# Where the last second-layer steps, the slots and two halves of weights stand ahead of an expert loop, and which branch is hinted

## The chip, the cores and the metric

One core of a Trainium2 chip runs the program. The metric is the device time of one execution in microseconds; lower is better. The times of the kernel before are a median and an interval of three timed runs, and beside them stands one profiled execution, from which all rows come.

## The reference

Attention of 8 batches with 8 heads, 576 queries and head size 64 over keys and values that are first averaged in groups of 8 (72 keys), then a mixture of experts over the 4608 tokens of width 512. Tokens with a skip score of 0 or less pass through.

```python
k_p = k.reshape(B, H, Sp, pool, D).mean(axis=3)          # v_p alike
scores = scale * np.matmul(q, k_p.transpose(0, 1, 3, 2))
attn = np.exp(scores - max); attn = attn / (attn.sum(-1) + 1e-9)
x = (attn @ v_p).transpose(0, 2, 1, 3).reshape(B * S, H * D)
do_compute = x @ w_skip > 0
e_idx = argmax(xc @ w_gate); gate_w = softmax(xc @ w_gate)[e_idx]
h = np.maximum(xc[mask] @ w1[e], 0.0)                    # for each of 8 experts
y[mask] = gate_w[mask, None] * (h @ w2[e])
out[do_compute] = xc + y
```

## The kernel before

A product in full precision is made of three products of rounded halves: a high half (`whi`, `xhi`, `hhi`, written by ScalarE) and a low half, the rest (`wlo`, `xlo`, `hlo`, written by VectorE or GpSimd). TensorE multiplies high by high, high by low and low by high. A low half of h is an operation of L512, a low half of a chunk of weights one of L555 (`low`).

The program has two stages. The first goes over 36 tiles of 128 tokens: attention, scores of the gate, and a table in memory that collects the tokens of each expert (the writes of L393, issued by GpSimd). Beside it, the tokens of one expert that are already known (two tiles) go through both of its layers: `products` takes the steps of its second layer one at a time, 16 of them at the end. A step is the three matmuls of L523 to L525 of 512 columns; eight steps (k from 0 to 7) fill one of two banks, psF[0] and mb. GpSimd's own list of small work is `gps`, a planner (`Paced`, L606 on) which in each slot of time picks between table writes and other work by due times; its constants say how many writes may stand in a row (L623). `later_low` (L646) numbers the 16 low halves of the weights and gives those up to 12 to it; the other three go to `rest`: VectorE makes 13 and 14 at a stop of `slots` (`late_lows`) and 15 behind the barrier (`lows`).

At the end of the first stage `slots` (L934) works out, on VectorE, which rows of the table belong to which unit of the second stage. It is a generator with stops. Its first part ends with the column of rows (L995) and the gather of these rows by GpSimd (L996), and stops with "". Its second part (from L1000) works out the kind (width) and ends of each unit, puts them through two small matmuls (L1020) and stops with "lows". Then the results are copied, and after another stop the gathered rows are transposed (L1028) and copied to `slot` and `gate` (L1029 on). What stands at the stops is in the loop over `slots` (L914 on): `products(.., 16)` goes on until 16 steps are left, `evacuate` writes halves of h that are waiting, `late_lows` are the two low halves of weights, and each `psum()` (that is, `spare`, L906) takes a bank and fills the time with KEEP = 6 matmuls that nobody reads (L909). The last call leaves SPARE = 10 steps over; they are handed to `experts`.

`experts` opens (L1059) with a barrier (`tc.tile_critical`) that every engine enters. Behind it each engine has a program of its own, with counted semaphores: `P` waits for a semaphore and takes from it, `V` adds. GpSimd gathers three tiles of tokens in the order of PLACES (2, 1, 0; L1182) and signals land2, land1, land0. TensorE runs the ten steps that are left, with steps 2 to 5 ahead of 0 and 1 (`steps[:6] = ...`), waits for the semaphore "lo" ahead of step 5, and behind steps 5, 6 and 7 (BETWEEN) transposes one tile of x each (L1339). ScalarE and VectorE split it into xhi (L1355) and xlo (`x_low`, L1395). VectorE's result of the two early tiles is `early` (L1389).

The units of the loop have one of five widths: 256, 288, 320, 352 or 384 columns. `far_width` (L1125) makes a copy of the first layer, `first`, for each width (96 matmuls, L1274 to L1276), behind a row of four compare-branches (L1132): if kind < 3, go to copy 0; if kind < 4, go to copy 1; and so on. In the code the copy stands right behind its branch, so a test that fails jumps over a copy. Each branch is given a hint: a mark at an earlier place in the instruction stream, from which the branch is announced. `widths_ahead` (L1148) sets such a mark under a test of the register that holds the kind of the unit to come; for the first unit it is called behind step n of 3, for the others in `tx`. The branch at the end of a copy (L1142) has a mark at the head of the copy.

At the very start, WARM = (24, 64) are 24 rounds of two small matmuls (L560) ahead of the first scores.

## Time and profile before

| | us |
|---|---|
| median of three timed runs | 503.99 (503.57 to 505.11) |
| profiled execution, its own time | 502.38 |
| its span on the core | 500.6 |
| PE busy | 478.2 |
| VectorE (DVE) busy | 291.8 |
| ScalarE (ACT) busy | 232.3 |
| GpSimd (POOL) busy | 214.2 |

The profiled execution takes 1.8 us more than its span, and 1.6 us less than the median of the timed runs. Times in rows are counted from the start of the span. The mean granted TensorE clock of the execution is 0.988 of full speed. PE is the array, PEld its loads of weights, PEq and PEldq the sequencer's own instructions; L1065 is the helper that all counted waits share, so the line of a wait is found from what follows it.

### The profile page before, as it was taken

The page shows a single profiled execution, that of the slowest core. Times are in us where ns is not written, and L with a number is a line of the kernel's source. Part 1 is how long each engine was busy: PE and PEld are TensorE (multiplying, and loading weights), DVE is VectorE, ACT ScalarE, POOL GpSimd, SP SyncE. Part 2 cuts the span into 40 slices and gives each one's busy share as a digit, 9 for nine tenths or more (in the row PEclk, how much of TensorE's full clock was granted, in tenths as well). Part 3 has the DMA queues.
Part 4 walks back from the last instruction along what each step waited for, and adds up shares of the span by engine and source line. Part 5 has one row for each costly group of instructions (what it writes and reads, how often), then busy time and mean ns, then how long its engine had stood idle before and what let it go on. Part 6 is the DMA issues. An engine that isn't in the chain of part 4 may idle for free. (4 is left out here: it accounts for less than half of the span.)

```text
span 500.6 us, 10706 instructions
## 1 busy us (share of the span) xinstructions
PE 478.2 (96%) x3290; PEld 437.8 (87%) x3291; DVE 291.8 (58%) x738; ACT 232.3 (46%) x584; POOL 214.2 (43%) x272
## 2 busy tenths in 40 slices
PE   7999899999999989999999997999999999999994
PEld 6899899898888779898989897989899898989893
DVE  4877988888697433566665758733556553322321
ACT  5668678897781023364544547522335242212110
POOL 3489369789886321152304023522022223323221
PEclk9999999999999989999999998999999999999998
DMA  8999799975511165557562637642415120101101
GB/s 252 379 388 392 307 352 388 340 250 192 192 65 44 36 231 210 190 178 270 167 231 85 201 130 263 238 142 63 151 74 180 64 62 21 63 21 60 40 3 39
DMA packets 35364, 87.04 MB, mean 174 GB/s; under 512 B 7246, under 2 KB 9550, under 8 KB 33536
## 3 DMA queue, kind: packets, MB, share of 16 engines
q1 hardware_dynamic: 27392, 71.62, 40.5%
q0 software_dynamic: 7936, 14.99, 8.9%
q8 instruction: 16, 0.26, 0.2%
q14 instruction: 20, 0.16, 0.1%
HBM read 73.25 MB, written 20.73 MB: 188 GB/s over the span
## 5 line engine op out<-in xcount | busy, mean ns | idle before, releaser
L1274 PE MATMUL psl<-xhi,w1hi 128*128 128x256 f32 (+3 forms) x384 | 113.3, 295 | 2.2 <-PEq L1065 2.2
L1275 PE MATMUL psl<-xlo,w1hi 128*128 128x256 f32 (+3 forms) x384 | 113.0, 294 | 0.0
L1276 PE MATMUL psl<-xhi,w1lo 128*128 128x256 f32 (+3 forms) x384 | 113.0, 294 | 0.0
L1187 POOL DMA_INDIRECT out<-ring,slot x36 | 37.3, 1035 | 157.0 <-POOLq L1065 154.5
L1365 ACT ACTIVATE hhi<-psl 128x256 fp32r<-128x256 f32 (+3 forms) x96 | 39.3, 409 | 118.4 <-ACTq L1065 114.2
L1423 DVE SCALAR_TENSOR_TENSOR hlo<-psl,hhi 128x256 fp32r<-128x256 f32 (+2 forms) x96 | 40.4, 422 | 64.3 <-DVEq L1065 61.6
L1274 PEld LDWEIGHTS psl<-xhi,w1hi 128*128 128x128 f32 x384 | 72.8, 189 | 3.3 <-issue 2.9
L1275 PEld LDWEIGHTS psl<-xlo,w1hi 128*128 128x128 f32 x384 | 72.7, 189 | 0.4
L1276 PEld LDWEIGHTS psl<-xhi,w1lo 128*128 128x128 f32 x384 | 72.7, 189 | 0.0
L285 ACT ACTIVATE e<-sc,mn 128x72 f32<-128x72 f32 x288 | 64.9, 344 | 13.2 <-DVE mn L279 12.9
L1182 POOL DMA_INDIRECT ring<-out,slot x39 | 42.7, 1096 | 23.5 <-issue 19.0
L1355 ACT ACTIVATE xhi<-psd 128x512 fp32r<-128x512 f32 x36 | 19.1, 598 | 70.9 <-ACTq L1065 70.9
L310 PE MATMUL o<-vbd,pT 128*128 128x148 f32 (+1 forms) x312 | 49.3, 298 | 2.5 <-DVE x L332 1.4
L310 PEld LDWEIGHTS o<-vbd,pT 128*128 128x128 f32 (+1 forms) x312 | 38.5, 179 | 5.4 <-ACT pT L297 1.8
L393 POOL DMA_INDIRECT table<-pay,r_di x36 | 35.9, 996 | 16.2 <-DVE p_mx L417 7.5
L1400 DVE TENSOR_TENSOR w2lo<-stage,w2hi 128x1024 fp32r<-128x1024 f32 x28 | 34.4, 1227 | 10.7 <-DVEq L1065 9.1
L1296 PE MATMUL psf<-w2hi,hhi 128*128 128x512 f32 x96 | 38.0, 395 | 0.0
L1297 PE MATMUL psf<-w2lo,hhi 128*128 128x512 f32 x96 | 37.4, 390 | 0.0
L1298 PE MATMUL psf<-w2hi,hlo 128*128 128x512 f32 x96 | 37.4, 390 | 0.0
L1181 POOL COPY ring<-gate 128x1 f32<-128x1 f32 x36 | 10.7, 298 | 58.4 <-DMA out<-ring,slot 49.7
L1297 PE MATMUL mb<-w2lo,hhi 128*128 128x512 f32 x88 | 34.3, 390 | 0.0
L1296 PE MATMUL mb<-w2hi,hhi 128*128 128x512 f32 x88 | 34.3, 390 | 0.0
(245 smaller groups left out, 986.9 us busy)
## 6 DMA issues: line engine op xcount, KB each, us to landing
stage<-in_w SPq DMA_DIRECT2D x64, 512.0 KB, 3.5
out<-x SPq DMA_DIRECT2D x36, 256.0 KB
stage<-in_k SPq DMA_DIRECT2D x7, 1152.0 KB
qt<-in_q SPq DMA_DIRECT2D x9, 512.0 KB
hhi<-in_vm SPq DMA_DIRECT2D x4, 1024.0 KB
hlo<-in_vm SPq DMA_DIRECT2D x3, 1024.0 KB
xhi<-in_q SPq DMA_DIRECT2D x4, 512.0 KB
xlo<-in_q SPq DMA_DIRECT2D x4, 512.0 KB
```

The lines of the kernel that those rows point to most:

```text
L285: nc.scalar.activation(ev[:, h // 2, k0:k0 + SP], sc[:, h * SP:(h + 1) * SP], AF.Exp, bias=mn[:, 4 * i + h:4 * i + h + 1], scale=-1.0)
L310: nc.tensor.matmul(o_[sl, g * 2 * VA:(g + 1) * 2 * VA], pT[:, 2 * a + g, sl], vbd[b % 2][:, 2 * a + g, :], start=(g == 0), stop=False)
L1182: g.indirect_dma_start(ring[:, s % 6, 0:D], None, out, bass.IndirectOffsetOnAxis(ap=slot[:, s:s + 1], axis=0), bounds_check=NTOK - 1, oob_ ...
L1187: g.indirect_dma_start(out, bass.IndirectOffsetOnAxis(ap=offsets, axis=0), ring[:, s % 6, 0:D], None, bounds_check=NTOK - 1, oob_is_err=Fa ...
L1274: t.matmul(ps, whi[0][:, k, w], xhi[:, k, xs], start=(k == 0), stop=False)
L1275: t.matmul(ps, whi[0][:, k, w], xlo[:, k, xs], start=False, stop=False)
L1276: last = t.matmul(ps, wlo[0][:, k, w], xhi[:, k, xs], start=False, stop=(k == 3))
L1296: t.matmul(ps, hhi[:, k, sl], whi[1][:, k, :], start=(k == 0), stop=False)
L1297: t.matmul(ps, hhi[:, k, sl], wlo[1][:, k, :], start=False, stop=False)
L1298: last = t.matmul(ps, hlo[:, k, sl], whi[1][:, k, :], start=False, stop=(k == 7))
L1365: a.activation(hhi[:, f, xs], psL[f % 3][:, xs], AF.Relu).then_inc(sem["act"], 1)
L1423: return v.scalar_tensor_tensor(out[:, f, :], psL[f % 3][:, xs], 0.0, hhi[:, f, xs].bitcast(F32), ALU.max, ALU.subtract)
```

## The change

Six edits, all ahead of the expert loop or at its head.

- Low halves of weights: 11 to 15 go to `rest` in place of 13 to 15. 11 and 12 are then `late_lows` and are made by GpSimd right behind the gather of L996, at the stop ""; 13 and 14 move from VectorE's place ahead of the barrier to its place behind the barrier, ahead of 15.
- At the stop "" the steps go on to 15 left in place of 16, and only then h is evacuated, until three of its halves are left; so the second part of `slots` stands behind the first low half of h. The stop behind L1020 now hands over a bank; there the other halves of h are evacuated, the steps go on to 12, and the fillers stand (KEEP is 4 and they come once).
- SPARE is 11 in place of 10: one more step stands behind the barrier. There steps 3 to 6 come ahead of 0 to 2, the transposes stand behind steps 6, 7 and 8, and the wait for "lo" is met ahead of three steps (n of 4, 5, 6) in place of one.
- `Paced` may put up to three large table writes in a row near the end in place of two.
- WARM is 26 in place of 24.
- The first unit's branches have one hint in place of four: if kind is over 2, a mark behind step n of 3 announces jumps[1].

```diff
@@ -62,11 +62,11 @@
 TWO = 1
 LOOPED = True
 PLACES = 2, 1, 0
-SPARE = 10
-BETWEEN = 5, 6, 7
-KEEP = 6
+SPARE = 11
+BETWEEN = 6, 7, 8
+KEEP = 4
 QUARTERS = 288, 320, 352, 384
-WARM, AGAIN = (24, 64), (42, 40)
+WARM, AGAIN = (26, 64), (42, 40)
 FIRST = [b * S // 128 for b in range(B)]
 SLOTS = 3 * (MAXU + 2)
 NO_TOKEN = 1 << 20
@@ -620,7 +620,7 @@
                     work = next((i for i in self.items if i[2] <= t), None)
                     write = next((i for i in self.writes if i[2] <= t), None)
                     if work and write:
-                        i = work if self.wrote > (t > NT - 7) or work[0] < write[0] and work[0] <= t else write
+                        i = work if self.wrote > 2 * (t > NT - 7) or work[0] < write[0] and work[0] <= t else write
                     else:
                         i = work or write
                     if i is None:
@@ -644,10 +644,10 @@
         rest = []
 
         def later_low(cc, i):
-            if cc * 2 + i > 12:
+            if cc * 2 + i > 10:
                 rest.append(lambda v: low(cc, i, v))
             else:
-                gps.add((now["t"] + 1, NT - 6, NT - 6, NT - 1, NT - 1)[max(cc - 2, 0)], wload(cc + 3) - 1 if cc < 3 else (NT - 3, NT - 1, NT + 9, NT + 9)[cc - 3],
+                gps.add((now["t"] + 1, NT - 6, NT - 6, NT - 1)[max(cc - 2, 0)], wload(cc + 3) - 1 if cc < 3 else (NT - 3, NT - 1, NT + 9)[cc - 3],
                         1.25, lambda: low(cc, i))
 
         def adds(b, ready, last):
@@ -901,27 +901,23 @@
                 clock["pe"] = max(clock["pe"], clock["dve"]) + 0.3
                 clock["dve"] = clock["pe"] + 0.3
         gps.take(NT + 99)
-        banks = []
-
-        def spare():
-            banks[:] = [ps_o.tile([128, 2, 512], F32, name="o")]
-            for _ in range(KEEP):
-                nc.tensor.matmul(banks[0][:, 1], hhi[:, 0, 0:128], whi[1][:, 0, :], start=True, stop=True)
-            return banks[0][:, 0].rearrange("p (i n) -> p i n", i=4)
-
         hhi, late_lows = bufs["hhi"], rest[:2]
         rest[:2] = []
+        spare = lambda: ps_o.tile([128, 2, 512], F32, name="o")
         for wait in slots(tc, nc, c, offs, table, near, bufs, out, fin, ap, spare):
             if wait == "":
-                products(NT * 99.0, 16)
+                for f in late_lows:
+                    f(nc.gpsimd)
+                products(NT * 99.0, 15)
+                while len(waiting) > 3:
+                    evacuate()
+                busy[0] = False
+            elif isinstance(wait, bass.AP):
                 while waiting:
                     evacuate()
                 products(NT * 99.0, 12)
-                busy[0] = False
-            elif wait == "lows":
-                for f in late_lows:
-                    f(nc.vector)
-                products(NT * 99.0, 11)
+                for _ in range(KEEP):
+                    nc.tensor.matmul(wait, hhi[:, 0, 0:128], whi[1][:, 0, :], start=True, stop=True)
             elif wait:
                 held = kinds(nc.scalar, fin["nti"])
             elif busy[0]:
@@ -1015,10 +1011,11 @@
     nc.vector.tensor_tensor(kind, kind, le1, ALU.mult)
     yield
     nc.vector.tensor_reduce(both[:, 0:1], kind, axis=AX.X, op=ALU.add)
-    tp = psum()
+    o = psum()
+    tp = o[:, 0].rearrange("p (i n) -> p i n", i=4)
     for i in range(2):
         nc.tensor.matmul(tp[0:1, 2 + i, 0:SLOTS], both[:SLOTS, i:i + 1], c["ident"][:SLOTS, :SLOTS], start=True, stop=True)
-    yield "lows"
+    yield o[:, 1]
     of_unit = tp[0:1, 2:4, 0:SLOTS].rearrange("p i (u s) -> p i u s", s=3)[:, :, :, 0]
     nc.vector.tensor_copy(nti[0:1, UNITS:2 * UNITS], of_unit[:, 1])
     nc.vector.tensor_scalar(nti[0:1, 0:UNITS], of_unit[:, 0], float(TWO), None, ALU.add)
@@ -1130,7 +1127,8 @@
             for i in range(len(QUARTERS)):
                 froms.append(nc.cur_bb)
                 jumps.append(e.br_cond(kind < TWO + i + 1, f"{name}_go{i}", f"{name}_not{i}"))
-                jumps[i].branch_hint(marks[i])
+                if i in marks:
+                    jumps[i].branch_hint(marks[i])
                 nc.switch_bb(f"{name}_not{i}")
             mark = e.mark_branch_hint_location()
             go(widths[-1])
@@ -1318,20 +1316,21 @@
                         second_short()
 
                 assert len(steps) == SPARE
-                steps[:6] = steps[2:6] + steps[:2]
+                steps[:7] = steps[3:7] + steps[:3]
                 loads = registers(t, nti)
                 held = next(loads)
-                marks, jumps = [], []
+                marks, jumps = {}, []
                 for n, (_, _, f) in enumerate(steps):
-                    if n == 5:
+                    i = int(not 4 <= n < 7)
+                    if not i:
                         P(t, "lo")
-                    i = int(not 4 <= n < 6)
                     m = f(psF[1 - i])
                     if m:
                         m.then_inc(sem["l2"], 1)
                     next(loads, None)
                     if n == 3:
-                        marks = widths_ahead(t, held[1])
+                        with t.If(t.snap(held[1], min_val=0, max_val=TWO + 4) > TWO + 1):
+                            marks = {1: t.mark_branch_hint_location()}
                     if n in BETWEEN:
                         i = PLACES[BETWEEN.index(n)]
                         P(t, f"land{i}")
```

## Rows read from the trace of the kernel before

A timeline's row has: start us, us, engine, line, operation, out<-in, xcount, and in brackets the idle time ahead of it with what released it.

**Rows 1.** page, part 1: busy us (share) xinstructions of each engine
```profile
PE 478.2 (96%) x3290; PEld 437.8 (87%) x3291; DVE 291.8 (58%) x738; ACT 232.3 (46%) x584; POOL 214.2 (43%) x272
```

**Rows 2.** waits of PE: line waited for, total us, times, longest us
```profile
PE psl L1274 <- PEq L1065: 2.2, 1, 2.2
```

**Rows 3.** timeline, PE, around the expert loop's first matmul
```profile
179.17 0.40 PE L525 MATMUL psf<-w2hi,hlo 128*128 128x512 f32 x1
...
181.81 0.60 PE L1274 MATMUL psl<-xhi,w1hi 128*128 128x320 f32 x1 [2.24 <-PEq L1065]
```

**Rows 4.** timeline, DVE: the last low part of x
```profile
179.04 0.69 DVE L1395 TENSOR_TENSOR xlo<-psd,xhi 128x512 fp32r<-128x512 f32 x1 [0.67 <-DVEq L1065]
```

**Rows 5.** lines L1132 and L1142, 140 to 200 us: branches, ns
```profile
L1132 PEldq COMPARE_BRANCH  x3: 79/380/2989, 177.9 to 181.5; - x3
...
L1142 PEldq COMPARE_BRANCH  x1: 2039/2039/2039, 194.8 to 194.8; - x1
```

**Rows 6.** windows behind the gap; columns by engine, then clock, DMA
```profile
181.70:185.10 3.40, 3.29 (x12) 3.33 (x13) 0.00 (x0) 0.00 (x0) 0.70 (x1) 0.50 0.74 233
...
185.10:188.50 3.40, 3.40 (x24) 3.40 (x24) 1.11 (x4) 0.87 (x2) 0.13 (x1) 1.00 1.02 402
```

**Rows 7.** timeline, PE, ahead of the barrier and behind it
```profile
163.21 0.39 PE L523 MATMUL mb<-w2hi,hhi 128*128 128x512 f32 x1
...
165.98 1.52 PE L909 MATMUL o<-w2hi,hhi 128*128 128x512 f32 x6
...
167.43 0.44 PE L1020 MATMUL o<-cfs,s_both 81*1 81x81 f32 x4
...
168.61 0.34 PE L1028 MATMUL o<-cfs,stage 81*128 81x81 f32 x2
...
169.31 0.40 PE L525 MATMUL mb<-w2hi,hlo 128*128 128x512 f32 x1
...
170.71 0.47 PE L523 MATMUL psf<-w2hi,hhi 128*128 128x512 f32 x1 [1.01 <-PE mb L525]
```

**Rows 8.** timeline, DVE, ahead of the barrier
```profile
160.06 0.16 DVE L995 TENSOR_TENSOR s_coli<-s_col 128x1 int32<-128x1 f32 x1
...
160.14 0.68 DVE L512 SCALAR_TENSOR_TENSOR hlo<-sc,hhi 128x512 fp32r<-128x512 f32 x1
...
163.16 1.29 DVE L512 SCALAR_TENSOR_TENSOR hlo<-pt,hhi 128x512 fp32r<-128x512 f32 x2 [2.34 <-ACT hhi L509]
...
166.54 1.28 DVE L555 TENSOR_TENSOR w2lo<-stage,w2hi 128x512 fp32r<-128x512 f32 x2
...
168.99 0.24 DVE L1029 CAST slot<-o 128x81 int32<-128x81 f32 x1 [0.81 <-PE o L1028]
```

**Rows 9.** line L1028, 140 to 200 us: PE's sequencer
```profile
L1028 PEldq EVENT_SEMAPHORE  x1: 51/51/51, 167.0 to 167.0; - x1
```

**Rows 10.** timeline, GpSimd (POOL), ahead of the barrier
```profile
151.71 1.30 POOL L555 TENSOR_TENSOR w2lo<-stage,w2hi 128x512 fp32r<-128x512 f32 x1
...
162.73 1.08 POOL L996 DMA_INDIRECT stage<-table,s_coli  x1 [2.18 <-issue]
```

**Rows 11.** timeline, PE, start of the program
```profile
1.75 5.38 PE L560 MATMUL o<-ring 128*64 128x64 f32 x48 [1.75 <-POOL ring L684]
...
8.95 0.51 PE L273 MATMUL sc<-kbd,qt 128*128 128x144 f32 x2 [0.71 <-ACT kbd L190]
```

**Rows 12.** timeline, PE: sets of transposes for x
```profile
174.92 0.60 PE L1339 MATMUL psd<-cfs,ring 128*128 128x128 f32 x4
...
175.28 0.48 PE L523 MATMUL psf<-w2hi,hhi 128*128 128x512 f32 x1
...
177.54 0.63 PE L1339 MATMUL psd<-cfs,ring 128*128 128x128 f32 x4
```

**Rows 13.** timelines of weight loads (PEld) and ScalarE (ACT)
```profile
161.82 0.19 PEld L502 LDWEIGHTS sc<-xlo,w1hi 128*128 128x128 f32 x1 [1.16 <-issue]
...
162.04 1.09 ACT L509 ACTIVATE hhi<-pt 128x512 fp32r<-128x512 f32 x2 [8.15 <-remote]
```

## The prediction

> **What bounds the kernel now.** I read the busy times first: TensorE (PE) is busy for 478.2 us of a span of 500.6 [rows 1]. Little but PE's idle time can be won, so I read the list of what PE waited for, and then the timeline at the place that the diff touches. One of its two longest waits, 2.2 us, stands at the first L1274, the first matmul of the expert loop [rows 2]. In the timeline the last product ahead of the loop starts at 179.17 and lasts 0.40, and the loop's first matmul starts at 181.81 [rows 3]: 2.24 us of nothing.
>
> The wait is named after the semaphore x of L1065, but x was there: the last x_low on VectorE (DVE) ends at 179.04 + 0.69 = 179.73 [rows 4]. What is late is PE's own sequencer. The view of line L1132 has three compare-branches of the tests that choose a width; they took 0.38, 2.99 and 0.08 [rows 5]. Kind is 3 here (320 columns), so the first two jump over a body of 96 matmuls with their loads and the third falls into the body behind it: the 2.99 is the second test, jumps[1]. Behind the gap the granted clock is 0.50 for 3.40 us: twelve matmuls in that window, 24 in the next equal one [rows 6]. At full clock twelve are 12/24 x 3.40 = 1.70; they took 3.29, so the low level cost 1.59.
>
> Ahead of this lies a barrier that all engines enter (L1059). PE arrives last, at 169.31 + 0.40 = 169.71 [rows 7]; DVE's three copies of the slots start at 168.99 and end by 169.5 [rows 8]. PE is last because of its order, not of data: the rows of the slots landed by 167.0, when PE's sequencer passed its wait for them [rows 9], but their transposes L1028 stand behind six filler matmuls, L1020 and a product, and start at 168.61 [rows 7].
>
> **The change part by part.** The sum is made along PE, from L523 at 163.21 to the barrier, then from the barrier to the first L1274.
>
> *The product that moves behind the barrier (SPARE 10 to 11).* Four steps of the second layer run from 163.21 to 165.98, 0.69 each [rows 7]. One less stands ahead of the barrier: -0.69. Behind the barrier it runs while PE would wait for the gathers and then for the slow branch, so it costs nothing there as long as that branch is slow.
>
> *Fillers, KEEP 6 to 4.* L909 is six matmuls from 165.98, and L1020 starts at 167.43: 1.45/6 = 0.24 with the change to the small matmul in it, about 0.225 without [rows 7]; two less are -0.45. They only fill PE while DVE gets ready, so this counts only if what stands behind them is ready sooner too.
>
> *Second part of the slots behind the first low half.* Today DVE writes the four low halves first and stands idle for 2.34 us ahead of the last two, which end at 163.16 + 1.29 = 164.45; the part lies between these and the two low halves of weights at 166.54, so it takes 2.1 at most [rows 8]. Behind the first low half (ends at 160.82) it runs from there to 162.9 at the latest, inside that idle time. L1020 then stands behind the first product, 163.21 + 0.69 = 163.9, and doesn't wait. L1020 itself stays on PE's path, only earlier in it: 0, between 0 and the -0.44 that it lasts [rows 7].
>
> *Two low halves of weights on GpSimd behind the gather L996.* Two operations leave GpSimd's row of table writes and two leave DVE (1.28 together [rows 8]). On GpSimd one takes 1.30 [rows 10]; without two of them the last writes start earlier, and L996 not before DVE's s_coli, written at 160.06 [rows 8]. L996 starts at 162.73 [rows 10], so it can gain some 1.5 us. That is worth nothing: in its new order PE gets to L1028 at 163.21 + 4 x 0.69 + 0.44 + 4 x 0.225 = 167.3, and the rows landed by 167.0 without it [rows 9]. The new low halves end near 162.73 - 1.5 + 1.08 + 2 x 1.30 = 164.9; the products that need them start at about 165.7 and 167.4. Cost 0, the cover being 0.8 to 2.5 us; if GpSimd were later by more, PE would wait for the rest.
>
> *Order of table writes.* Up to three writes in a row in place of two: the same operations, on an engine that isn't last. 0. *WARM 24 to 26* adds four passes of 5.38/48 = 0.11, 0.45 in all, ahead of a wait of 0.71 for kbd that takes them up [rows 11]. 0.
>
> Sum to the barrier: -0.69 - 0.45 = **-1.14**.
>
> *Behind the barrier.* PE restarts at 170.71, 1.00 after its arrival, and goes through six steps to the first transposes at 174.92, 0.70 each; the third set starts at 177.54 [rows 7, 12]. A set moves PE on by 175.28 - 174.92 = 0.36. With one step more ahead of them the third stands at 170.71 + 9 x 0.70 + 2 x 0.36 = 177.73, 0.19 later against the barrier than now (where it comes later than its own sum, 177.03, and so has a wait in it), and so does x (179.92 on the old scale). PE's sequencer isn't behind its array here: the first of the three tests is reached at 177.9 with transposes and two steps still queued [rows 5]. So the slow branch, not x, still decides, and 1.8 us of it hide the 0.19. The two added waits for "lo" (n of 4 and 5) have behind them only steps on PE; DVE restarts with PE, at about 170.7 on the old scale, and its three low halves at 1.28/2 = 0.64 each [rows 8] are done by 172.7; the first of these waits is met after four steps, at 173.5. DVE's next work, early(0), waits for PE anyway; SP's weight loads wait for DVE's signal behind these halves and for GpSimd's behind the third gather, which comes last (its transposes start at 177.54 [rows 12]).
>
> *The other hint.* Before, four hints name the branch that is logically taken; now one names jumps[1] when kind is over 2, which is the slow one. The bounds: 0 if the code of jumps[1]'s target is asked for no sooner; -2.61 (2.99 to the first test's 0.38 [rows 5]) less what x then limits. The nearest row is the branch of L1142 at the loop body's end: it had a hint 13 us ahead and took 2.04 all the same, 0.95 less than the slow one [rows 5]. That hint stood in the very body whose end it names; jumps[1] is reached right behind the jump of the first test, with hardly time between. I take -0.2.
>
> [...]
>
> Total -1.14 - 0.2 = -1.34. The profiled execution took 502.38 (span 500.6), so it would take 501.04; the three timed runs have a median of 503.99, 1.61 above it, and there the forecast is **502.65**. PE-bound work behind it moves as a whole.
>
> **The rivals.** *B: the hint works.* Then x decides: the first L1274 about 0.3 behind x, 179.92 + 0.3 - 1.14 = 179.1 in place of 181.81 - 1.14 = 180.7, -1.6. PE's gap shrinks to some 0.4, and if the clock then stays up, -1.59 more. 503.99 - 1.14 - 1.6 - 1.59 = 499.65; 501.25 if the clock falls anyway. For it: the hint names the branch that is slow. Against: the 2.04.
>
> *C: a new wait takes the place.* PE and ScalarE show a stop that nothing in the trace releases: a load of weights at 161.82 after 1.16 us of nothing, and ScalarE held for the same matmuls until 162.04 [rows 13]. If such a stop comes in the changed run alone, its 1.2 us eat the gain: 503.9. The other way to C is DVE's second part being held up while GpSimd computes beside it; if it ends 1.3 later (one operation of GpSimd [rows 10]) L1020 and all behind it on PE come up to 1.3 later: again 503.9. Against: it ends by 162.9, when GpSimd's low halves have only begun.
> [...]
>
> *D: slower.* One more code load is exposed. The branch of L1142 takes 2.04 unseen only because matmuls are queued ahead of it [rows 5]. If the loop's head moves in the code so that such a load falls where nothing is queued, it costs 2.99, and -1.34 turns to +1.65: 505.6, or 507.2 with a lowered clock behind it. It decides from the point where PE's instructions ahead of the loop don't cancel: +8 (WARM), -4 (KEEP), -6 (tests and hints), +2 (waits) is 0, which speaks against it.
>
> **How the numbers follow.** Forecast A 0.50, B 0.27, C 0.15, D 0.08. A measurement here tells 0.3% apart, 1.5 us. A's own range is 501.4 to 503.7 (the hint from 0 to -0.95, L1020 from 0 to -0.44, the stop of C in one of the two kernels), and its -1.34 lies just inside the bound: two fifths of A are faster. Faster: 0.20 + 0.27 = 0.47; same: 0.30 + 0.15 = 0.45; slower 0.08. The range takes in A, C and most of B: 499.6 to 504.6.
>
> **What would show it.** PE's arrival at the barrier 1.1 us earlier against the first L523; L1020 behind the first product without a wait; DVE's second part ahead of the second low half; the first L1274 about 12.1 us behind PE's arrival, as now, with a branch of 2.0 to 3.0 at L1132 ahead of it. A branch under 0.5 there and no stretch at 0.50 behind it is B; L1020 waiting for s_both is C. The prediction is wrong if the rows, not PE, end last at the barrier, or if the loop itself changes length.

## The result and the profile after

The changed kernel is slower: 510.73 us, median of four timed runs (510.51 to 511.19), against 504.17 (503.57 to 505.11) for four runs of the kernel before. The ratio is 1.0142, interval 1.0116 to 1.0167. The forecast was 502.65, its range 499.6 to 504.6; the time lies 6.1 us above the upper end. The profiled execution after took 510.55 us, 8.2 us more than the profiled execution before; its span is 508.7. The ratios and intervals, here and in the experiments, leave out executions over 1.5% above the fastest of their kernel (three of nine of `after_two`, one of eleven of `spare13_fill_golate`, and one near 950 us each in `before_hint_golate` and in the kernel before of set 1), whereas the medians count every execution and the ranges leave out only the two near 950.

Part 1 of the page of the kernel after (busy us, share, instructions) answers to [rows 1]:

```profile
PE 477.4 (94%) x3292; PEld 436.0 (86%) x3293; DVE 295.5 (58%) x738; ACT 232.7 (46%) x584; POOL 214.9 (42%) x272
```

PE does the same work and is idle for 8.9 us more. VectorE is busy for 3.7 us more, though the change takes two operations away from its stretch ahead of the barrier and puts as many behind it. The waits of PE in the kernel after (line waited for: total us, times, longest us) answer to [rows 2]:

```profile
PE psl L1272 <- PEq L1062: 3.5, 2, 2.5
PE o L1017 <- DVE s_both L1013: 3.3, 1, 3.3
...
PE psf L1294 <- PEq L1062: 1.3, 1, 1.3
```

The first wait is the old one (L1272 was L1274). The second is new, and it is the one that my rival C named. The third stands at the end of the first loop body. PE's timeline of the kernel after, from the first product to the loop, answers to [rows 3, 7]:

```profile
164.58 0.39 PE L523 MATMUL mb<-w2hi,hhi 128*128 128x512 f32 x1
...
168.74 0.70 PE L1017 MATMUL o<-cfs,s_both 81*1 81x81 f32 x4 [3.31 <-DVE s_both L1013]
169.37 0.80 PE L523 MATMUL mb<-w2hi,hhi 128*128 128x512 f32 x1
...
172.73 1.07 PE L920 MATMUL o<-w2hi,hhi 128*128 128x512 f32 x4
174.16 0.45 PE L1025 MATMUL o<-cfs,stage 81*128 81x81 f32 x2 [0.36 <-DVE nti L1021]
...
176.35 0.47 PE L523 MATMUL psf<-w2hi,hhi 128*128 128x512 f32 x1 [1.00 <-PE mb L525]
...
188.35 0.39 PE L1272 MATMUL psl<-xhi,w1hi 128*128 128x320 f32 x1 [2.54 <-PEq L1062]
```

Why s_both is late stands in the timelines of VectorE and of GpSimd (POOL) of the kernel after; they answer to [rows 8, 10]:

```profile
163.18 0.16 DVE L991 TENSOR_TENSOR s_coli<-s_col 128x1 int32<-128x1 f32 x1
163.26 0.69 DVE L512 SCALAR_TENSOR_TENSOR hlo<-sc,hhi 128x512 fp32r<-128x512 f32 x1
...
164.59 3.31 DVE L1003 TENSOR_TENSOR s_odd<-s_odd,s_three 128x8 int32<-128x8 int32 x1
167.93 0.17 DVE L1005 TENSOR_TENSOR s_none<-s_none,s_odd 128x8 f32<-128x8 f32 x1
```

```profile
164.27 1.07 POOL L992 DMA_INDIRECT stage<-table,s_coli  x1 [2.26 <-DVE s_short L999]
165.37 2.49 POOL L555 TENSOR_TENSOR w2lo<-stage,w2hi 128x512 fp32r<-128x512 f32 x2
176.92 1.60 POOL L1180 DMA_INDIRECT ring<-out,slot  x1 [9.06 <-issue]
```

L1003 works on 8 elements a partition, as its neighbours do, which take 0.17. It took 3.31 and ended at 167.90; GpSimd's two low halves ended at 165.37 + 2.49 = 167.86. In the kernel before the same operation took 0.16:

```profile
165.66 0.16 DVE L1007 TENSOR_TENSOR s_odd<-s_odd,s_three 128x8 int32<-128x8 int32 x1
```

The windows of the kernel after (length; busy time of PE, PEld, DVE, ACT, POOL; granted clock; DMA) show PE's clock behind its wait:

```profile
165.40:168.80 3.40, 0.09 (x2) 0.06 (x2) 3.33 (x8) 0.00 (x0) 2.46 (x2) 0.96 0.15 34
168.80:172.20 3.40, 3.40 (x11) 2.60 (x12) 1.69 (x3) 0.00 (x0) 0.00 (x0) 0.54 0.00 0
172.20:175.60 3.40, 2.79 (x12) 1.67 (x11) 0.72 (x5) 0.00 (x0) 0.00 (x0) 1.00 0.00 0
```

Behind 3.3 us of nothing the granted clock was 0.54 for 3.40 us, and 1.00 in the next window. The three steps from 169.37 to 172.73 took 3.36; at 0.69 a step [rows 7] they take 2.07, so 1.29 is lost there.

The branches of the kernel after, 140 to 205 us (count: shortest/median/longest ns, and when), answer to [rows 5]:

```profile
L1129 PEldq COMPARE_BRANCH  x3: 75/391/3276, 184.2 to 187.9; - x3
...
L1140 PEldq COMPARE_BRANCH  x1: 3759/3759/3759, 201.4 to 201.4; - x1
```

| stretch along the path, us | before | after | more |
|---|---|---|---|
| start to the L390 at 121 us (VectorE's operation that makes a tile's routes) | 121.26 | 121.59 | 0.33 |
| from there to the last L390 | 33.93 | 36.46 | 2.53 |
| last L390 to the first psf product behind the barrier (the restart) | 15.52 | 18.30 | 2.78 |
| from there to the loop's first matmul | 11.09 | 12.00 | 0.91 |
| the loop to the end | 318.76 | 320.38 | 1.62 |

The five add up to 8.17. My sum covered the third and the fourth line: -1.14 and, with the hint, -0.2. From the first L523 to the barrier's other side the third line holds 3.31 (wait at L1017) + 1.29 (clock) + 0.26 (L1017 itself, 0.70 in place of 0.44) + 0.36 (L1025) - 1.14 (the forecast gain) = 4.08 of the 4.27 by which that piece grew. The rest of the line, 1.49 less, lies ahead of the first L523. All of it is the stop of PE [rows 13] that the trace of before has there and this one has not: in before, four steps from one matmul to the next took 1.97 where they take 0.12 each elsewhere.

```profile
160.08 0.28 PE L502 MATMUL sc<-xlo,w1hi 128*128 128x256 f32 x1
...
162.05 0.28 PE L503 MATMUL sc<-xhi,w1lo 128*128 128x256 f32 x1
```

### The profile page after: what moved, and what is told of

It reads as the page before. It is cut to its first block, busy times and chain, and to the rows that moved or that the text cites. A ratio compares the mean times of both kernels' runs of the same rounds, so it can differ in the third digit from the quotient of the medians.

```text
span 508.7 us, 10710 instructions
## 1 busy us (share of the span) xinstructions
PE 477.4 (94%) x3292; PEld 436.0 (86%) x3293; DVE 295.5 (58%) x738; ACT 232.7 (46%) x584; POOL 214.9 (42%) x272
## 5 line engine op out<-in xcount | busy, mean ns | idle before, releaser
L1272 PE MATMUL psl<-xhi,w1hi 128*128 128x256 f32 (+3 forms) x384 | 113.3, 295 | 3.5 <-PEq L1062 3.5
L1274 PE MATMUL psl<-xhi,w1lo 128*128 128x256 f32 (+3 forms) x384 | 113.0, 294 | 0.0
L1185 POOL DMA_INDIRECT out<-ring,slot x36 | 38.5, 1070 | 157.6 <-POOLq L1062 154.8
L1272 PEld LDWEIGHTS psl<-xhi,w1hi 128*128 128x128 f32 x384 | 72.7, 189 | 4.7 <-issue 4.3
L1274 PEld LDWEIGHTS psl<-xhi,w1lo 128*128 128x128 f32 x384 | 72.8, 190 | 0.0
L1294 PE MATMUL psf<-w2hi,hhi 128*128 128x512 f32 x96 | 38.1, 396 | 1.3 <-PEq L1062 1.3
L1294 PE MATMUL mb<-w2hi,hhi 128*128 128x512 f32 x88 | 34.3, 390 | 0.0
```

Source lines behind the costliest of these rows:

```text
L1185: g.indirect_dma_start(out, bass.IndirectOffsetOnAxis(ap=offsets, axis=0), ring[:, s % 6, 0:D], None, bounds_check=NTOK - 1, oob_is_err=Fa ...
L1272: t.matmul(ps, whi[0][:, k, w], xhi[:, k, xs], start=(k == 0), stop=False)
L1274: last = t.matmul(ps, wlo[0][:, k, w], xhi[:, k, xs], start=False, stop=(k == 3))
L1294: t.matmul(ps, hhi[:, k, sl], whi[1][:, k, :], start=(k == 0), stop=False)
```

## The experiments

All kernels of one set ran on the same chip and share the runs of the kernel before, whose medians were 504.10, 502.56, 502.84, 502.62 and 504.09 in the five sets. "Edit" is against the kernel after or before, as the name begins; `dve_lows` and `spare13` are of the kernel after. A ratio is not the quotient of the two medians and can differ from it: `dve_lows_b` has 0.9961, and its medians give 0.9979.

| set | kernel | median (range), us | ratio to before |
|---|---|---|---|
| 1 | after_dve_lows | 505.38 (503.42 to 508.14) | 1.0017 (0.9995 to 1.0039) |
| 1 | after_one_low | 508.13 (504.57 to 510.05) | 1.0074 (1.0049 to 1.0099) |
| 1 | after_shift6 | 511.29 (509.81 to 511.97) | 1.0140 (1.0096 to 1.0184) |
| 1 | before_hint | 508.67 (507.42 to 510.14) | 1.0092 (1.0060 to 1.0125) |
| 2 | dve_lows_two | 502.41 (500.24 to 503.05) | 0.9986 (0.9965 to 1.0007) |
| 2 | before_hint_bare | 503.07 (500.24 to 505.76) | 1.0007 (0.9981 to 1.0033) |
| 2 | before_hint_golate | 506.18 (503.28 to 506.78) | 1.0056 (1.0026 to 1.0087) |
| 2 | before_dead80 | 503.11 (501.89 to 504.47) | 1.0004 (0.9983 to 1.0026) |
| 3 | after_two | 506.10 (499.67 to 508.61) | 1.0003 (0.9960 to 1.0047) |
| 3 | dve_lows_b | 501.80 (500.38 to 503.64) | 0.9961 (0.9938 to 0.9985) |
| 3 | dve_lows_two_b | 501.55 (500.15 to 504.14) | 0.9979 (0.9947 to 1.0010) |
| 3 | spare13 | 502.90 (500.01 to 507.47) | 0.9988 (0.9951 to 1.0026) |
| 4 | after_c | 505.94 (501.89 to 507.38) | 1.0056 (1.0028 to 1.0083) |
| 4 | spare13_fill | 500.70 (499.91 to 502.28) | 0.9957 (0.9936 to 0.9977) |
| 4 | spare13_fill_golate | 502.58 (500.43 to 508.83) | 0.9984 (0.9953 to 1.0014) |
| 5 | before_three | 504.66 (501.57 to 505.34) | 1.0005 (0.9983 to 1.0027) |
| 5 | before_spare11 | 504.76 (503.28 to 506.74) | 1.0006 (0.9987 to 1.0026) |
| 5 | spare13_fill2 | 508.81 (506.24 to 509.83) | 1.0092 (1.0059 to 1.0124) |

### What holds L1003

The theory: GpSimd's two halves of weights hold VectorE's operation on two inputs in SBUF. The rival: the gather ahead of them does it. The first kernel has VectorE make the two halves, behind the second part.

```diff
-                for f in late_lows:
-                    f(nc.gpsimd)
...
+                for f in late_lows:
+                    f(nc.vector)
                 products(NT * 99.0, 12)
```

> The changed kernel, but its two late low halves of weights are made by VectorE, behind the last low half of h, and GpSimd makes none behind the gather. Theory A (GpSimd's two halves hold VectorE's L1003, an operation on two SBUF inputs, for as long as they last): L1003 takes under 0.2 us in place of 3.31, TensorE's wait at L1017 falls from 3.31 to under 1, and no stretch of lowered clock follows it; 510.7 - 2.6 - 1.3 + up to 0.6 for halves that are now made later = 506.2 to 507.4. Rival B (the issue of the gather L992 holds L1003, and the halves only happen to stand behind it): L1003 still takes about 0.75, up to the gather's end; the time is nearly the same, 506.5 to 507.5, so the operation's length tells the two apart. Rival C (a stop that has nothing to do with GpSimd): L1003 still takes about 3 us, 510.7.

VectorE's and GpSimd's timelines of after_dve_lows:

```profile
164.98 0.16 DVE L1003 TENSOR_TENSOR s_odd<-s_odd,s_three 128x8 int32<-128x8 int32 x1
```

```profile
164.75 1.07 POOL L992 DMA_INDIRECT stage<-table,s_coli  x1 [2.31 <-DVE s_short L999]
```

L1003 stands 0.23 into the gather's issue and takes 0.16; in dve_lows_b (below) it stands 0.32 into it, as in after, and takes 0.16 too. The gather alone doesn't hold it, and the rival falls. PE's wait at L1017 went from 3.31 to 1.06, and the ratio from 1.0142 to 1.0017: the one edit that stood at cost 0 in the prediction is worth 1.25%, 6.3 us, by these two ratios, and all the rest of the change together nearly nothing. They come from different sets, though with nearly the same time of before (504.17 and 504.10); how far the size holds is taken up at after_c.

One of the two halves on GpSimd, the other on VectorE:

```diff
-                for f in late_lows:
-                    f(nc.gpsimd)
+                late_lows[0](nc.gpsimd)
...
+                late_lows[1](nc.vector)
                 products(NT * 99.0, 12)
```

> The changed kernel with one of the two late halves on GpSimd behind the gather, and the other on VectorE behind the last low half of h. Theory A (held for as long as GpSimd's halves last): L1003 takes 3.31 - 1.25 = 2.06 us, TensorE's wait at L1017 about 2.1, 510.7 - 1.25 = 509.4, up to 1.3 less if the clock stays up. Rivals B (the gather's issue) and C (neither): L1003 as long as in the changed kernel or as long as with no half on GpSimd, nothing in between.

That L1003 would be held by one half was a miss: the gather came late (165.65), and the second part was done by then. The hold fell on another operation. VectorE's and GpSimd's timelines of after_one_low:

```profile
166.70 1.89 DVE L555 TENSOR_TENSOR w2lo<-stage,w2hi 128x512 fp32r<-128x512 f32 x1
```

```profile
166.75 1.27 POOL L555 TENSOR_TENSOR w2lo<-stage,w2hi 128x512 fp32r<-128x512 f32 x1
```

VectorE's own half, 0.69 elsewhere [rows 8: 1.28 for two], took 1.89, and ended 0.57 behind GpSimd's. So it is not L1003 alone: two different operations of VectorE on two inputs in SBUF were held beside GpSimd's halves, one beside one half for 1.2, the other beside two in a row for 3.15. One that reads an input from PSUM was not held: in after_shift6 (below) GpSimd makes both halves too, but the gather came 0.8 later behind s_coli (1.87 against 1.09), the second part was done by 164.44, and a low half of h took its usual 0.68 beside them. VectorE's and GpSimd's timelines of after_shift6:

```profile
165.57 0.68 DVE L512 SCALAR_TENSOR_TENSOR hlo<-sc,hhi 128x512 fp32r<-128x512 f32 x1
```

```profile
165.08 2.54 POOL L555 TENSOR_TENSOR w2lo<-stage,w2hi 128x512 fp32r<-128x512 f32 x2
```

The length of the hold in the kernel after is 3.15, through two instructions of GpSimd without an end of VectorE's between them, and it starts 0.78 ahead of the first half. These are measured; how one engine holds the other is not shown.

The changed kernel with the old rule for table writes, and the changed kernel once more without any edit:

```diff
-  ... self.wrote > 2 * (t > NT - 7) or ...
+  ... self.wrote > (t > NT - 7) or ...
```

> The changed kernel with the old rule for table writes (two in a row), its two late halves still on GpSimd behind the gather. Theory A (the halves on GpSimd are what costs): it stays some 4 to 5 us slower than dve_lows_two_b on the same chip, near 507, and an operation of VectorE on two SBUF inputs stands held for 1 us or more beside the halves. Theory S (the rule of three is what costs, by delaying the routes and so bringing VectorE's second part beside the halves): most of the loss is gone, 503 to 504, within 1 us of dve_lows_two_b.

> The changed kernel itself once more, on the chip and in the hour of the two kernels beside it. Theory A (the cost is a meeting of GpSimd's two halves with VectorE's second part of the slots, which depends on when the gather L992 comes against that part): where the profile shows L1003, or another operation on two SBUF inputs, held for 2.5 to 3.3 us, TensorE's restart stands 17.5 to 18.5 us behind the last L390, and where none is held, 15 to 16; the runs spread over 3 us or more, as those of after_two did (499.7 to 508.6), with a median 3 to 7 us above the kernel before. Rival S (besides that, the rule of three delays the routes): the last L390 stands 36 us or more behind the routes at 121; without it 32.9, as dve_lows_b showed.

VectorE's timeline of after_two:

```profile
160.83 3.31 DVE L1003 TENSOR_TENSOR s_odd<-s_odd,s_three 128x8 int32<-128x8 int32 x1
```

In after_c it is again 3.31, at 160.51. The first half starts 0.79 behind L1003 in after_two and 0.80 in after_c. In both, PE waits 3.30 at L1017 and the clock falls behind it: the granted clock is 0.74 from 165 to 168.4 us in after_two and 0.50 from 164 to 168 us in after_c. The piece from the last L390 to the restart took 18.46 in after_two and 19.64 in after_c, longer than expected of the latter, since the lower clock lasted for all three steps and the fillers. Against dve_lows_b (0.9961), after_c (1.0056) stands 0.95% higher, 4.8 us, though in another set. after_two scatters from 499.67 to 508.61, and its interval settles nothing by itself: beside dve_lows_two_b of its own set, which differs by the two halves alone (0.9979, 0.9947 to 1.0010), the two intervals overlap, although in the traces the way from the last L390 to the restart is 18.46 against 14.13. Of the kernels that differ by the halves only, and within one set, the times part clearly for after_one_low alone (1.0074 against 1.0017 of after_dve_lows).

The hold itself is shown by the traces. Its size in time is less sure: one and the same kernel stands at 1.0142 in the first comparison and at 1.0056 in set 4, and the two intervals are apart. The halves explain 1.25% and 0.95% by the two pairs; why the first comparison lies 0.9% above set 4 is not shown.

### The head of the loop

The hint alone, in the kernel before; first with five added pairs of semaphore instructions ahead of the loop, then bare:

```diff
-                        marks = widths_ahead(t, held[1])
+                        with t.If(t.snap(held[1], min_val=0, max_val=TWO + 4) > TWO + 1):
+                            marks = {1: t.mark_branch_hint_location()}
...
+                for _ in range(5):
+                    V(t, "pad")
+                    P(t, "pad")
                 units(t, held, unit)
```

> The kernel before with the new hint alone (one, on jumps[1] when kind is over 2, in place of four), and ten instructions of padding ahead of the loop so that the loop's code lies within one instruction of where it was. Theory H0 (the hint does not bring the code sooner): the second test of L1132 still takes 2.9 to 3.3 us, 504.2 within 0.8. Rival H1 (the hint works): under 0.5 us, the gap ahead of the first L1274 shrinks from 2.24 to some 0.5, and with the clock up behind it 504.2 - 1.7 - 1.6 = 500.9.

> The kernel before with the new hint alone and without padding. Theory D (the code that jumps[1] leads to is fetched only when TensorE gets there, and the fetch takes long when the weight loads of SyncE have started first; in before_hint the padding brought TensorE there 0.5 us behind the first packet of the loads in place of 1.0 ahead of it): without padding the branch comes ahead of the loads again, takes 2.9 to 3.3 us as in the kernel before, and the time is 504.1 within 0.8. Rival H (the new hint itself does harm): the branch takes over 4 us again, 507 to 509.

The bare hint gives 1.0007: nothing in time. Its branch took 4.55, and not 2.9 to 3.3 as expected, and started 0.94 behind SP's first load. The profiled execution was the longest of its ten (505.76), PE's clock was low behind the restart (granted 0.50 from 171.0 to 174.4, 1.28 a step in place of 0.69), and so the branch came late. With the pairs the time got worse, which neither theory had; the five pairs take PE's sequencer 1.6 us ahead of the branch. Branches of before_hint, and SP's timeline of it:

```profile
L1132 PEldq COMPARE_BRANCH  x3: 75/391/5758, 179.3 to 185.6; - x3
```

```profile
178.25 4.43 SPq L1168 DMA_DIRECT2D stage<-in_w  x8
```

The slow branch starts at 179.77, 1.53 behind SP's first load of weights. A packet of an instruction queue starts at 183.20, behind those loads; that it holds the code behind the jump is my reading. In the kernel before, branch and loads start together, at 178.42 and 178.41, and such a packet, of 16 KB, starts 0.64 behind the branch. So I formed a second theory: a hint brings nothing, and the price of the jump is set by whether weight loads stand ahead of this packet. The test holds the loads back in before_hint, by moving VectorE's signal "go" behind its last x_low:

```diff
-                v.engine_nop().then_inc(sem["go"], 1)
                 held = kinds(v, nti)
...
                 m.then_inc(sem["x"], 1)
+                v.engine_nop().then_inc(sem["go"], 1)
                 early(1)
```

> The kernel before_hint (new hint and ten instructions of padding), but VectorE's signal that lets SyncE start the weight loads comes behind its last low half of x in place of ahead of the loop, some 1.4 us later. Theory D (the branch's fetch waits behind the weight loads' packets): the fetch starts under 1 us behind the branch, the branch takes 2.9 to 3.3 us in place of 5.76, and the time falls from 508.7 by 2.5 to 3, to some 506; the loads of 4 MB have slack for 1.4 us. Rivals H (the hint) and K (the padding, by its place in the code): the branch takes 5 to 6 us still, 508.7.

Branches of before_hint_golate, and SP's timeline of it:

```profile
L1132 PEldq COMPARE_BRANCH  x3: 75/391/3416, 178.4 to 182.3; - x3
```

```profile
179.58 6.05 SPq L1168 DMA_DIRECT2D stage<-in_w  x8
```

5.76 became 3.42, with the packet 0.69 behind the branch. The ratio fell from 1.0092 to 1.0056, 1.8 us where 2.5 to 3 were expected; with these intervals that difference shows nothing.

The rival to the whole view was that the code behind the jump is asked for ahead of the jump, at a point that depends on where the tests stand in the code. 80 instructions that are jumped over move the tests to another place:

```diff
+                        with t.If(t.snap(held[1], min_val=0, max_val=TWO + 5) > TWO + 4):
+                            for _ in range(80):
+                                V(t, "pad")
```

> [...] Rival F (a block is asked for only by the jump into it): 2.9 to 3.3 us as before, 504.1 + 0.2 for the jump.

The branch took 3.05 with its packet 0.62 behind it, and the time is the same (1.0004). In both places that were tried, 2.99 and 3.05 for the branch, the packet starts behind the branch (0.64 and 0.62) and not ahead of it.

The changed kernel with three pairs ahead of the loop was to show whether the branch at the loop body's end (3.76 in after, 2.04 in before) depends on its place in the code:

```diff
+                for _ in range(3):
+                    V(t, "pad")
+                    P(t, "pad")
                 units(t, held, unit)
```

> [...] The three pairs themselves cost nothing, being behind TensorE's last products and ahead of the slow branch L1129.

The pairs did cost: they take the sequencer 0.95, and the branch at the head came 0.91 behind the first load and took 4.67. That at the body's end no longer stands out (0.38). In its profile L1003 also took only 0.16, and the wait at L1017 was 1.07, so the 1.0140 of this kernel can't be put down to the hold: against the trace of after_dve_lows, the way from the restart to the loop is 2.15 longer and the loop 0.95. The branch at the body's end took 0.38 in dve_lows_two and 3.27 in dve_lows_two_b, which are the same kernel, so its place in the code doesn't decide. What does is open.

### What the rest of the change is worth

The kernel after with VectorE's halves and the old rule for writes, twice; and with the new rule once more:

```diff
-                for f in late_lows:
-                    f(nc.gpsimd)
...
+                for f in late_lows:
+                    f(nc.vector)
                 products(NT * 99.0, 12)
...
-  ... self.wrote > 2 * (t > NT - 7) or ...
+  ... self.wrote > (t > NT - 7) or ...
```

> The changed kernel with its two late low halves on VectorE (as in the experiment after_dve_lows) and with the old rule for table writes, two in a row in place of three. Theory S (the packets of GpSimd's table writes hold back TensorE's completion signals, and the longer rows of writes make more of these stops; in the kernels run so far the last routes L390 stand 33.9 us behind those at 121 with the old rule and 36.0 to 36.6 with the new one): that distance falls from 36.6 to about 34, and the time from 505.4 by up to 2.3, to 503.1. Rival L (it is the two halves that left GpSimd's row, whatever the rule): the distance stays at 36 or more, 505.4. Rival N (the distance is noise): anywhere between 33.9 and 36.6, and the time follows it.

> The kernel dve_lows_two once more, beside dve_lows_b on the same chip. Theory S: 0.3% faster than dve_lows_b; rival N: the same within 0.1%. Against the kernel before: about 0.7 us faster (0.9986 as measured earlier), TensorE's restart behind the barrier 1.3 us earlier against the last L390 and 0.8 of it given back between the restart and the first matmul of the loop.

> The kernel after_dve_lows once more, on the same chip as dve_lows_two_b, which differs by the rule for table writes alone (three in a row here). Theory S: the last routes L390 come 2 us or more later behind those at 121 than in dve_lows_two_b, and the time is 1.5 to 2.5 us longer. Rival N (the difference between the two earlier runs was one of chips): the distance from 121 to the last L390 is the same within 0.5 us, and so is the time.

From the last L390 to the restart these take 14.16, 14.13 and 14.17, against 15.52 before. That is 1.36 less, but it is not the prediction's 1.14: the 15.52 of before holds the stop of 1.5 ahead of the first L523, and from the first L523 to the restart these three take 7.62 to 7.70, against 7.50 before. Nearer neighbours are three kernels that are as before up to the barrier and have no stop in their traces: before_hint_golate takes 15.51 from the last L390 to the restart, before_hint_bare 15.95, before_dead80 16.05. PE waits 1.34 to 1.79 there for the rows of the slots. PE's timeline of before_dead80:

```profile
168.71 0.42 PE L1028 MATMUL o<-cfs,stage 81*128 81x81 f32 x2 [1.79 <-DMA stage<-table,s_coli]
```

Their last table write starts 5.2 to 5.5 behind the last L390 and the gather 4.1 to 4.5 behind s_coli; in the three kernels here it is 3.0 and 1.1. So what the rest of the change brings, 1.3 to 1.9, goes with the earlier rows. PE waits at two new places in them, 0.2 at L1017 and 0.36 at L1025. VectorE's and PE's timelines of dve_lows_b:

```profile
166.99 0.17 DVE L1020 CAST nti<-o 1x27 int32<-1x27 f32 x1 [1.14 <-PE o L920]
```

```profile
167.31 0.45 PE L1025 MATMUL o<-cfs,stage 81*128 81x81 f32 x2 [0.36 <-DVE nti L1021]
```

The copy of the kinds waits for the four fillers, which write to the same tile, and PE waits for the copy. Behind the barrier they take 11.89, 12.08 and 11.73 to the loop's first matmul, against 11.09, so 0.6 to 1.0 is given back. The rule made no difference: from the L390 at 121 us to the last is 32.90 in all three. In time they stand at 0.9961 to 0.9986, and only the interval of dve_lows_b leaves 1 out.

The rule alone, and the step alone that moves behind the barrier (with VectorE's two halves), in the kernel before:

```diff
+  ... self.wrote > 2 * (t > NT - 7) or ...
```

> The kernel before with the new rule for table writes alone (up to three in a row near the end in place of two). Rival N (in an hour without late signals of TensorE the rule changes nothing that counts): the last routes L390 stand 32.9 us behind those at 121, and the time is within 0.8 us of the kernel before. Theory S (the rule delays the routes): 34 to 36.5 us, and 1 to 2.5 us slower; if TensorE's completion signals come late in this hour, as they did in the first session, with more of them than the four in the kernel before.

```diff
-SPARE = 10
-BETWEEN = 5, 6, 7
+SPARE = 11
+BETWEEN = 6, 7, 8
...
-        hhi, late_lows = bufs["hhi"], rest[:2]
-        rest[:2] = []
+        hhi, late_lows = bufs["hhi"], []
...
-                steps[:6] = steps[2:6] + steps[:2]
+                steps[:7] = steps[3:7] + steps[:3]
...
-                    if n == 5:
+                    i = int(not 4 <= n < 7)
+                    if not i:
                         P(t, "lo")
-                    i = int(not 4 <= n < 6)
```

> The kernel before with the moved step alone: 11 steps behind the barrier in place of 10, in the new order, the three last low halves of weights on VectorE behind the barrier in place of one, six fillers as before. Theory X (what stands behind the barrier is paid: the three halves of VectorE hold up GpSimd's first gather behind the barrier, 1.59 us in place of 1.07 as in every kernel with three halves there, and the branch comes later with it): the restart comes 0.6 to 1.2 us earlier against the last L390, the way from the restart to the loop's first matmul is 11.8 to 12.0 us in place of 11.1, and the time is within 0.5 us of the kernel before. Rival Y (as I forecast: the step costs nothing there): that way is 11.1 to 11.3 us, the time 0.7 to 1.1 us shorter.

before_three: VectorE's L390 at 121 us and the last:

```profile
121.07 0.16 DVE L390 TENSOR_TENSOR r_di<-r_ds,mb 128x7 int32<-128x7 f32 x1
...
157.32 0.16 DVE L390 TENSOR_TENSOR r_di<-r_ds,mb 128x3 int32<-128x3 f32 x1 [0.22 <-DMA table<-pay,r_di]
```

That is 36.25, 2.3 more than before, and yet the restart comes only 0.63 later (171.34) and the time is the same (1.0005): this trace has no stop ahead of the first L523.

before_spare11, which has the stop, gains 0.1 ahead of the barrier (15.41; 0.23 from the first L523 on), not 0.69: PE gets there sooner and waits 1.56 there in place of 1.01, because the slots' copies on VectorE now end last. And it loses behind it. GpSimd's and PE's timelines of before_spare11:

```profile
171.67 1.59 POOL L1181 DMA_INDIRECT ring<-out,slot  x1 [7.38 <-issue]
```

```profile
171.10 0.47 PE L523 MATMUL psf<-w2hi,hhi 128*128 128x512 f32 x1 [1.56 <-SPq L1058]
...
183.22 0.38 PE L1273 MATMUL psl<-xhi,w1hi 128*128 128x320 f32 x1 [2.60 <-PEq L1064]
```

From restart to loop 12.12, against 11.09. The first gather takes 1.59. It does so (1.59 to 1.61) in all 14 kernels in which VectorE makes three halves behind the barrier, and takes 1.07 in all 6 in which it makes one: 171.28 in the kernel before, when that one half, 170.63 to 171.32, is all but over. The hold of L1003 would be the other way round here, VectorE holding GpSimd; that the halves are the cause rests on the split of 14 to 6 and on this run.

### More steps behind the barrier

A version of my own: the kernel after with VectorE's halves at the stop ahead of the transposes, 13 steps behind the barrier and the old rule; then (spare13_fill) with five matmuls that nobody reads on PE just ahead of the barrier, in a bank of their own, the last three lines of the diff; then with "go" late as above.

```diff
-SPARE = 11
-BETWEEN = 6, 7, 8
+SPARE = 13
+BETWEEN = 5, 7, 8
...
-                steps[:7] = steps[3:7] + steps[:3]
+                steps[:9] = steps[5:9] + steps[:5]
...
+        bank = ps_s.tile([128, 512], F32, name="sc")
+        for _ in range(5):
+            nc.tensor.matmul(bank, hhi[:, 0, 0:128], whi[1][:, 0, :], start=True, stop=True)
```

> The kernel dve_lows_two with 13 steps of the second layer behind the barrier in place of 11 (transposes behind steps 5, 7 and 8), and the two halves on VectorE behind the copies of the units' kinds. Theory Q (what stands behind the last transposes on TensorE hides the slow branch; two steps more there cost nothing, and two less stand ahead of the barrier, where the gathered rows then bound the time): the restart comes 1.3 to 1.8 us earlier against the last L390 than in dve_lows_two, the way from the restart to the loop's first matmul stays within 0.3 us of 11.9, and the time is 1.2 us less, 0.3% under dve_lows_two_b. Rival R (the two steps are paid behind the barrier, as the one in the changed kernel was): from the restart to the loop 13.2 us, the same time as dve_lows_two_b.

> The kernel spare13 with five more filler matmuls on TensorE behind the transposes L1025, in a bank of their own, so that TensorE is busy until about when VectorE reaches the barrier. Theory G (in spare13 the gap of 2.13 us ahead of the restart brought the clock down, the first five steps behind it took 1.28 us each in place of 0.69, and so the slow branch came 1.2 us behind the first packet of the weight loads in place of 1.0 ahead of it and took 7.55 us): the gap falls to about 1.1, the steps take 0.69 each from the first on, the branch is reached some 0.5 us ahead of the first packet or more and takes 3 to 3.5 us; 502.9 - 3 = 500. Rival V (the two steps behind the barrier are what makes the branch late): the branch is again behind the loads and takes over 4.5 us, 502 to 503.

> The kernel spare13_fill, with VectorE's signal that lets the weight loads start behind its last low half of x in place of ahead of the loop. Theory D (the block of code for jumps[1] waits behind the loads' packets wherever these are first): the fetch starts within 0.8 us of the branch in every profile, the branch takes 3.0 to 3.5 us, the runs spread less than those of spare13 (500.0 to 507.5), and the median is 499.5 to 500.5, 0.5% under the kernel before. Rival W (the loads are needed by then: a later start is paid in the loop): the loop, from its first matmul to the end, is 1 us or more longer than in spare13_fill.

PE's timelines of spare13 and of spare13_fill at the restart and at the loop:

```profile
167.56 0.77 PE L523 MATMUL psf<-w2hi,hhi 128*128 128x512 f32 x1 [2.13 <-SPq L1056]
...
185.81 0.60 PE L1272 MATMUL psl<-xhi,w1hi 128*128 128x320 f32 x1 [4.93 <-PEq L1062]
```

```profile
168.10 0.47 PE L523 MATMUL psf<-w2hi,hhi 128*128 128x512 f32 x1 [1.01 <-PE sc L928]
...
179.76 0.39 PE L1275 MATMUL psl<-xhi,w1hi 128*128 128x320 f32 x1 [0.87 <-PEq L1065]
```

Without fillers PE restarts 0.12 sooner behind the last L390 (13.42 against 13.54) and takes 6.59 longer from there to the loop (18.25 against 11.66). The profiled execution of spare13 took 506.99, and its median is 502.90. Its 2.13 of waiting are followed by steps of 1.28 in place of 0.69 (granted clock 0.50 from 169.4 to 172.8); so the branch comes 2.18 behind the first load (175.70) and takes 7.55. With fillers the steps keep 0.69, branch (176.31) and load (176.28) start together, the branch takes 3.06, and no lower clock follows (1.00 from 179.7 to 183.1). This kernel is the fastest of its set, 0.9957 (0.9936 to 0.9977). Late loads add nothing to it: in the trace the branch takes 3.29 and the loop 322.2 in place of 319.2. That fits a price of the late loads in the loop, but 1.03 of the 3.0 is a longer wait at the first body's end, and the rest is not traced.

The same with the two halves at the earlier stop and four fillers:

```diff
+                for f in late_lows:
+                    f(nc.vector)
                 products(NT * 99.0, 13)
```

> The fastest kernel so far, spare13_fill (0.9957 of the kernel before), with the two late halves of VectorE ahead of the copies of the units' kinds, where VectorE stood idle for 1.2 us, and four fillers behind the transposes in place of five. If VectorE bounds the barrier there: the copies of the slots start 0.4 us earlier against the last L390 and the restart with them, the branch takes 3.0 to 3.5 us ahead of the loads, and the median is 0.9947 to 0.9957 of the kernel before. If the gathered rows bound it instead: the same time as spare13_fill within 0.1%, 0.9957.

It took 1.0092, but its trace has 38.2 from the L390 at 121 us to the last and a wait of PE of 4.4 at L374, well ahead of the edit. So the place of the halves isn't settled by it, and the gain of spare13_fill is shown in one set only, one whose traces have no such waits.

### The routes

The second line of the table of stretches (2.53) was in no term of mine. The signals of PE come late in some traces. Timelines of before and of after, the last transpose and the ScalarE operation that waits for it:

```profile
129.51 0.27 PE L293 MATMUL pt<-cfs,e 128*128 128x128 f32 x1
...
129.88 0.70 ACT L297 ACTIVATE pT<-pt 128x640 f32<-128x640 f32 x1 [0.83 <-PE pt L293]
```

```profile
129.85 0.27 PE L293 MATMUL pt<-cfs,e 128*128 128x128 f32 x1
...
131.22 0.70 ACT L297 ACTIVATE pT<-pt 128x640 f32<-128x640 f32 x1 [1.84 <-PE sc L273]
```

ScalarE starts 0.10 behind the transpose's end in the one and 1.10 behind it in the other. Between 100 and 170 us the semaphore records hold 4 signals of PE over 0.1 us late in before, 9 in after, 9 in before_three and none in after_c; in after, most of them come while packets of GpSimd's table writes are under way. From the L390 at 121 us to the last is 33.93, 36.46, 36.25 and 32.91 in these four. The traces of sets 2 to 4 have no such signals and take 32.9 with either rule; each of those of sets 1 and 5 has 5 or more. Sets 1 and 3 ran on one chip, so the chip alone isn't it. The stop that I put into rival C [rows 13] goes with one of these: the signal of a matmul that ended at 159.06 came at 162.02. before_hint and before_spare11 have the same signal late (161.75 and 162.53) and the same stop.

## Why the prediction was wrong

*What bounds the kernel*: right. PE is the bound, and its gap at the loop's head comes from the second test's jump, in every kernel here (2.99 us in before, 7.55 in spare13).

*Two halves of weights on GpSimd, "Cost 0"*: this is the step that failed. Counted from s_coli, my times held: I had the gather 1.2 and the halves 2.25 behind it, and they came 1.09 and 2.19 behind. I asked only when the halves' results would be needed, and not what VectorE does in these 2.5 us. By my own bounds the second part ended up to 2.84 behind s_coli, so the two overlapped, and rival C's "Against" (the halves have "only begun") doesn't follow from them. It started earlier than that, even, for L1003 was caught 0.78 ahead of the halves, under the gather's last part. C's price of 1.3 was one operation of GpSimd; it is two of them and the gather's rest, 3.15, and 1.55 of lowered clock behind it. C was given 0.15 and no loss.

*The sum to the barrier, -1.14*: once the halves are away the total has the size (1.3 to 1.9 less than kernels like before without the stop), but by luck, for neither term comes out in the traces as it was summed. From the first L523 to the restart, where the sum was made, nothing is gained (7.62 to 7.70 against 7.50). The step alone gave 0.23 there in before_spare11. "Some 1.5 us. That is worth nothing", of the earlier gather, is where the gain lies: "because of its order, not of data" was read from a trace in which PE's stop of 1.5 had hidden its wait for the rows, and without the stop that wait is 1.34 to 1.79.

*Behind the barrier, "costs nothing"*: wrong by about 0.9. I had the third transposes 0.19 later against the restart; in after they are 183.78 - 176.35 = 7.43 behind it and in before 6.83, so 0.60 later. 0.53 of that is the first gather, 1.60 in place of 1.07, beside VectorE's three halves. And the slow branch doesn't hide it: the branch comes 8.26 behind the restart in place of 7.71, because the sequencer gets to the tests only behind its wait for those tokens. The cover that I named moved with the work that it was to hide.

*The hint, -0.2*: 0 (the bare hint stands at 1.0007). The L1142 row by which I leaned to a gain was a branch whose length changes from trace to trace without any edit to its hint (0.29 to 4.93), and rival B with its 0.27 falls.

*Fillers, WARM, order of writes*: the two fillers' own time held (1.07 for four in place of 1.52 for six, -0.45), but 0.36 of it comes back as PE's wait at L1025, since the copy that L1025 waits for now waits for the fillers. The L390 at 121 us lies at 120.76 to 122.67 in all these traces, before at 121.26 and after at 121.59, so WARM can't be told from nothing. The rule of three is 1.0005 in time.

*Rival D*: in after's profile 1.3 of the 3.76 of the branch at the body's end is exposed (the wait at psf L1294), most of the loop's 1.62. The exposed branch is there, not by the place of the code, and it was not the main part: taking the halves off GpSimd did away with nearly all of the difference (1.0142 and 1.0017, in two sets), and 0.95% of it by after_c and dve_lows_b.

## What to carry to other kernels

Work that is moved to an engine that has time is not free until one has listed what the neighbouring engine does in the same microseconds, and on which memories: a VectorE operation of 0.16 on two inputs in SBUF stood still for 3.31 beside two GpSimd operations, and it was the one that PE waited for. Price a wait of PE with the clock behind it (here 1.55 on top of 3.31), and where a wait can't be avoided, matmuls that nobody reads may be cheaper than restarting sooner (11.66 from the restart to the loop with them in spare13_fill, 18.25 without in spare13). A stall that is to hide new work must be checked for whether it starts later itself. And one trace is one execution: the stop in mine hid a wait for rows that three others have, and a term that I put at nothing was where the gain lay.

## What the hardware showed that I had not expected

- An operation of VectorE on two inputs in SBUF, 0.16 elsewhere, took 3.31 in after, after_two and after_c beside two GpSimd operations that follow each other within 0.1 us. It ended only with the second, and it stood still already 0.78 to 0.80 ahead of the first, under a gather beside which alone it takes 0.16. Why is open.
- The second test's jump took 2.99 to 3.42 where it started together with the weight loads or ahead of them (before, before_dead80, spare13_fill, after, spare13_fill_golate, before_hint_golate), and 4.55, 4.67, 5.76 and 7.55 where it started 0.94, 0.91, 1.53 and 2.18 behind them (before_hint_bare, after_shift6, before_hint, spare13). A hint changed none of it: in after its mark ran 6.6 ahead of the branch, which took 3.28.
- A signal of PE can come up to 3 us behind the modelled end of its matmul (159.06 and 162.02 in before), in some sets and not in others; in after most of the late ones come while table writes are under way. Which sets is open.
